# A fused attention and two-expert kernel: VectorE closes the old chunk before it finishes the new one

## The chip, the cores and the metric

The kernel runs on one core of one Trainium2 chip. The metric is device time in microseconds (us) for one execution. Engines are called as in the profile: PE (TensorE), PEld (its weight loads), DVE (VectorE), ACT (ScalarE), POOL (GpSimd) and SP (SyncE, which here issues DMAs). L340 means line 340 of the kernel before.

## The reference

The program computes a windowed causal attention with a linear bias (4 batches, 8 heads, 576 positions, head size 64), reshapes its output to 2304 tokens of 512 features, and sends these through two pairs of dense layers. Only the first pair matters here:

```python
def _moe_ref(x, w_in, w_out, a, b):
    h = x @ w_in                       # 2304 x 512 by 512 x 2048
    h2 = h * h
    h3 = h2 * h
    P = a[0] + a[1] * h + a[2] * h2 + a[3] * h3
    Q = 1.0 + np.abs(b[0]) * np.abs(h) + np.abs(b[1]) * h2
    g = P / (Q + 1e-06)
    return g @ w_out                   # 2304 x 2048 by 2048 x 512
```

The second pair has the same sizes, `g = h` where `h > 0` and `exp(h) - 1` elsewhere.

## The kernel before, in words

Full precision on PE comes from splitting every operand into a rounded high part and a low remainder, and multiplying hi·hi, lo·hi and hi·lo. So a product of 128 rows by a contraction of 512 takes 12 matmuls.

The tokens of the first pair are cut into five blocks (512, 512, 512, 256, 512). In each block the 2048 hidden features are cut into 16 chunks of 128, so there are 80 chunks, counted c or s over all blocks, and f = 0 to 15 in a block. For every chunk PE makes a first product (`gemm1`, L287: 12 matmuls into the bank `h`) and a second one (`gemm2_T`, L725: 12 matmuls that add to four `acc` banks). Between the two stands `rational`, the quotient P/(Q + 1e-6), on 128 x 512 tiles.

One call `rational(c)` works on two chunks at once, the new chunk c and the old chunk c - 1:

- ACT makes of the new `h`: its square h2 (L311), qa = |b0|·|h| (L312), ee = a0 + a1·h (L313), and a2 + a3·h in place of h (L314). Then the reciprocal of Q as exp(-ln Q): L325 and L326, into `rr`.
- DVE makes for the old chunk the rounded quotient hi = ee0·rr0 (L319), then qq0 = Q·hi (L331), then the remainder ee0 - qq0 (L339). POOL (DVE for the first four chunks) multiplies that by rr0 (L340): this is the low part of the quotient.
- DVE makes for the new chunk Q without its 1 (L322), h2 times the rest of the polynomial (L336, into `h`), and adds that to ee (L337).

The tiles `ee` and `qq` exist twice and lie in a token block of `xT` that is used up; a chunk takes the pair of the chunk before the last. So L313 of the next chunk writes the tile that POOL reads in L340, and waits for it. `h2` exists once, so L311 of the next chunk waits for L336. The order on each engine is the order in which the program text issues (`manual_schedule`). PE runs ahead: in the loop over s it issues `gemm1(s)`, then `gemm2_T(s - 3)`, then `rational(s)` is issued to the other engines.

Between these passes stand jobs on weights. In block 0 they convert this pair's weights (`conv_step`, L138, L148, L156 to L162). In blocks 1 and 2 all chunks but f = 0, 8 and 15 have two "joins": 26 chunks, 52 joins. A join takes half of a weight slice of the second pair: ACT scales its high words (L130), DVE shifts its low words (L138), then ORs both (L800), SP stores the result and loads a further half. The first join of a chunk stands between L319 and L322; the second one's shift stands before L331, and its L800 (which needs an L130 that ACT makes after L326) after L331. At f = 15, ACT and DVE also split the next block's x into hi and lo (`split_x`, L268 and L269), and three chunks later ACT copies the four `acc` banks of the finished block (L732).

After the 80 chunks the second pair of layers runs with a planner of its own, which the diff doesn't touch.

Of the kernel before, what the change touches and what calls it, by code (L numbers as in the profile page):

```python
# [13 lines left out]
ALU = mybir.AluOpType  # L14
# [30 lines left out]
def kernel(  # L45
# [13 lines left out]
    nc = tc.nc  # L59
# [178 lines left out]
    def width(c):  # L238
        return BL[c // KF][1]

    def row1(tag, c):

        t0, n = BL[c // KF]
        if tag in BESIDE:
            return xT[:, BESIDE.index(tag), t0:t0 + n]
        where, c0 = ROW1[tag]
        return SPACE[where][:, c0:c0 + n]
# [5 lines left out]
    def bank(n, shape, name):  # L253
        return psum.tile(shape, F32, tag=f"b{n}", name=name)
# [47 lines left out]
    def rational(c, old=True, beside=3 * (lambda: None,), after=lambda: None):  # L302


        old = old and c - 1 in q_t
        new = c in h_t
        if new:
            h = h_t.pop(c)
            h2, ee, qq, rr = [row1(nm, c) for nm in ("h2", f"ee{c % 2}", f"qq{c % 2}", f"rr{c % 2}")]
            qa = bank(6, [P, width(c)], "qa") if c > 3 else qq  # L310
            nc.scalar.activation(out=h2, in_=h, func=AF.Square)  # L311
            nc.scalar.activation(out=qa, in_=h, func=AF.Abs, scale=b_abs[:, 0:1])  # L312
            nc.scalar.activation(out=ee, in_=h, func=AF.Identity, scale=a_sb[:, 1:2], bias=a_sb[:, 0:1])  # L313
            nc.scalar.activation(out=h, in_=h, func=AF.Identity, scale=a_sb[:, 3:4], bias=a_sb[:, 2:3])  # L314
        if old:
            qq0, ee0, rr0 = q_t.pop(c - 1)
            hi, low = row1(f"ghi{c % 3}", c - 1), row1(f"glo{c % 3}", c - 1)
            g_t[c - 1] = (hi, low)
            nc.vector.tensor_tensor(out=hi, in0=ee0, in1=rr0, op=ALU.mult)  # L319
        beside[0]()  # L320
        if new:
            nc.vector.scalar_tensor_tensor(  # L322
                out=qq, in0=h2, scalar=b_abs[:, 1:2], in1=qa, op0=ALU.mult, op1=ALU.add
            )
            nc.scalar.activation(out=rr, in_=qq, func=AF.Ln, bias=c_q)  # L325
            nc.scalar.activation(out=rr, in_=rr, func=AF.Exp, scale=-1.0)  # L326
            q_t[c] = (qq, ee, rr)
        after()
        beside[1]()
        if old:  # L330
            nc.vector.scalar_tensor_tensor(  # L331
                out=qq0, in0=qq0, scalar=EPSC, in1=hi.bitcast(F32), op0=ALU.add, op1=ALU.mult
            )
        beside[2]()
        if new:
            nc.vector.tensor_tensor(out=h, in0=h2, in1=h, op=ALU.mult)  # L336
            nc.vector.tensor_tensor(out=ee, in0=ee, in1=h, op=ALU.add)  # L337
        if old:
            nc.vector.tensor_tensor(out=ee0, in0=ee0, in1=qq0, op=ALU.subtract)  # L339
            (nc.gpsimd if c > 4 else nc.vector).tensor_tensor(out=low, in0=ee0, in1=rr0, op=ALU.mult)  # L340


    def attention():
        with ExitStack() as es:
# [339 lines left out]
            for t in range(first, NU + 2):  # L684
                if 0 <= t < 12:
                    load_some(2)
                if t == NU - 1:
                    x1[0] = split_x(0, "DADA")
                    ahead = early()
                for step, late in STEPS:  # L690
                    run(step, t + late)
                    if t < NU - 1 or not 0 <= t + late < NU:
                        continue

                    for _ in range(AHEAD.get((t + late, step), 0)):
                        next(ahead, None)
                    if (t + late, step) in CONV_AFTER:
                        conv_step(to_conv, to_conv[0] not in LATE[4:], eng="D")
                    if (t + late, step) == FIRST["r0"]:
                        rational(0)  # L700
                    if (t + late, step) == FIRST["r1"]:
                        rational(1, old=False)
                if t == 0:
                    nc.sync.dma_start(out=a_sb, in_=moe_a.partition_broadcast(P))
                    nc.sync.dma_start(out=b_raw, in_=moe_b.partition_broadcast(P))
                if t == 2:
                    nc.scalar.activation(out=b_abs, in_=b_raw, func=AF.Abs)
# [3 lines left out]
    def experts():  # L711
# [519 lines left out]
        def prepare(s):  # L1231
            f = s - LAST
            if f == 3:
                load_wi(0)
            if f == 14:
                load_wi(1)
                for e in raw_ones(0):
                    load_raw(0, e)

            def copies():  # L1240
                for fn in AT_ACT.get(f, []):
                    fn()

            def next_one():
                if f >= 3 and AT_DVE:
                    AT_DVE.pop(0)()
            rational(s, beside=(lambda: None, next_one, next_one), after=copies)
# [89 lines left out]
```

## Time and profile before

| | |
|---|---|
| runs | 980.41, 980.75, 981.29 us; median 980.75 |
| the profiled execution | 981.41 us, of which 979.6 us span from the first to the last instruction |
| PE busy | 927.1 us (95%) |
| DVE busy | 824.5 us (84%) |
| ACT busy | 709.4 us (72%) |
| POOL busy | 192.8 us (20%) |
| mean granted clock of PE | 0.995 of full speed |

The times are of a whole execution. The span leaves out 1.8 us around it. PE is busy nearly always, but the share is a mean: the attention, the five blocks and the second pair have different limits. In the trace the blocks lie about here: block 0 from 150 to 230 us, block 1 to 341, block 2 to 455, block 3 to 510 and block 4 to 597.

### The profile page before, as it was taken

Reading aid. Unit: us, or ns where it says so; the run is one execution under the profiler, and the core shown is the slowest. Engines: PE = TensorE matmul, PEld = TensorE weight load, DVE = VectorE, ACT = ScalarE, POOL = GpSimd, SP = SyncE. Lnnn points to the kernel's source line nnn. Section 1 sums busy time; section 2 is a strip of 40 time slices with the busy share of each in tenths; the row PEclk is TensorE's granted clock in tenths of the full one; section 3 lists DMA queues with packets and bytes.
Section 4 is the critical chain, followed back from the end, with each engine's and each line's share of the span. In section 5 each row is a group of like instructions: output and inputs, shape, how many; then the busy total and the mean of one; then the engine's idle time right before and its main releaser. Section 6 shows DMA issues by size and latency. Waiting matters only on the chain.

```text
span 979.6 us, 15614 instructions
## 1 busy us (share of the span) xinstructions
PE 927.1 (95%) x5110; PEld 775.1 (79%) x5110; DVE 824.5 (84%) x1773; ACT 709.4 (72%) x1510; POOL 192.8 (20%) x238
## 2 busy tenths in 40 slices
PE   9999999999888797878999999999999999999998
PEld 6777777877666586657988888899998999899897
DVE  7899999999888888887789998999978878787653
ACT  6999998778666676666787787767776657676553
POOL 4566650222222122222222321000000000000000
PEclk9999999999999999998999999999999999999999
DMA  8999851011333223230000012435444232343201
GB/s 163 226 261 216 216 152 41 1 33 33 102 92 105 89 82 113 81 114 22 1 2 32 1 64 77 148 121 194 129 147 145 85 118 76 124 155 109 75 1 65
DMA packets 112561, 98.28 MB, mean 100 GB/s; under 512 B 62816, under 2 KB 86368, under 8 KB 112480
## 3 DMA queue, kind: packets, MB, share of 16 engines
q1 hardware_dynamic: 109936, 96.57, 33.6%
q10 hardware_dynamic: 2544, 0.72, 0.4%
q8 instruction: 40, 0.66, 0.3%
q14 instruction: 41, 0.34, 0.1%
HBM read 79.96 MB, written 17.30 MB: 99 GB/s over the span
## 4 chain that ended last, share of the span: by engine, by line
PE 59%; DVE 21%; issue 6%; ACT 6%; POOL 4%; DMA 2%; POOLq 0%; DVEq 0%; ACTq 0%
PE acc L951 20%; PE m L935 18%; PE acc L725 9%; PE h L287 8%; POOL space_g L340 4%; DVE h L336 2%; DVE xT L337 2%; DVE xT L339 2%; ACT xT L313 2%; DVE half L138 2%; ACT h L314 1%; DVE pr_wi L518 1%; DMA joined_wi<-space_u 1%; DVE cvt L148 1%; DVE pr_wo L518 1%
## 5 line engine op out<-in xcount | busy, mean ns | idle before, releaser
L725 PE MATMUL acc<-space_g,w_wo 128*128 128x512 f32 (+1 forms) x960 | 222.7, 375 | 32.1 <-POOL space_g L340 30.4
L725 PEld LDWEIGHTS acc<-space_g,w_wo 128*128 128x128 f32 x960 | 168.8, 190 | 74.1 <-POOL space_g L340 43.2
L340 POOL TENSOR_TENSOR space_g<-xT,space_r 128x512 fp32r<-128x512 f32 (+1 forms) x76 | 106.3, 1399 | 348.0 <-DVE xT L339 281.1
L313 ACT ACTIVATE xT<-h,a_sb 128x512 f32<-128x512 f32 (+1 forms) x80 | 59.0, 738 | 82.7 <-POOL space_g L340 81.6
L951 PE MATMUL acc<-op_wo,space_g 128*128 128x512 f32 x432 | 108.3, 393 | 0.0
L287 PE MATMUL h<-space_qa,w_wi 128*128 128x512 f32 (+1 forms) x320 | 92.3, 372 | 4.0 <-ACT space_qa L268 3.3
L951 PEld LDWEIGHTS acc<-op_wo,space_g 128*128 128x128 f32 x432 | 80.4, 188 | 14.7
L287 PE MATMUL h<-space_qb,w_wi 128*128 128x512 f32 (+1 forms) x240 | 76.6, 374 | 3.8 <-DVE space_qb L269 3.6
L997 ACT ACTIVATE space_u<-space_r 128x384 f32<-128x384 f32 x48 | 25.1, 522 | 75.3 <-DVE space_r L991 74.3
L287 PE MATMUL h<-space_ta,w_wi 128*128 128x512 f32 (+1 forms) x240 | 77.0, 375 | 2.3 <-DVE space_ta L269 2.3
L935 PE MATMUL m<-xo_wi,op_wi 128*128 128x384 f32 x336 | 77.3, 337 | 0.0
L935 PE MATMUL m<-xo_wo,op_wi 128*128 128x384 f32 x336 | 76.4, 335 | 0.0
L287 PEld LDWEIGHTS h<-space_qa,w_wi 128*128 128x128 f32 x320 | 57.4, 189 | 15.5 <-ACT space_qa L268 4.8
L336 DVE TENSOR_TENSOR h<-space_u,h 128x512 f32<-128x512 f32 (+1 forms) x80 | 51.0, 637 | 16.8 <-ACT h L314 16.7
L935 PEld LDWEIGHTS m<-xo_wo,op_wi 128*128 128x128 f32 x336 | 60.9, 188 | 4.1
L325 ACT ACTIVATE space_r<-xT,c_q 128x512 f32<-128x512 f32 (+1 forms) x80 | 54.2, 678 | 11.2 <-DVE xT L322 8.6
L935 PEld LDWEIGHTS m<-xo_wi,op_wi 128*128 128x128 f32 x336 | 60.6, 188 | 0.0
L322 DVE SCALAR_TENSOR_TENSOR xT<-space_u,b_abs,qa 128x512 f32<-128x512 f32 (+1 forms) x76 | 52.1, 686 | 10.0 <-ACT qa L312 10.0
L287 PE MATMUL h<-space_bi,w_wi 128*128 128x512 f32 (+1 forms) x160 | 59.6, 373 | 0.0
L311 ACT ACTIVATE space_u<-h 128x512 f32<-128x512 f32 (+1 forms) x80 | 43.7, 546 | 21.6 <-DVE h L336 19.0
L1001 ACT ACTIVATE space_u<-space_u,c_m 128x384 f32<-128x384 f32 x96 | 57.5, 610 | 1.6
L331 DVE SCALAR_TENSOR_TENSOR xT<-xT,space_g 128x512 f32<-128x512 f32 (+1 forms) x80 | 57.9, 723 | 0.1
(187 smaller groups left out, 2158.7 us busy)
## 6 DMA issues: line engine op xcount, KB each, us to landing
space_qa<-joined_wo SPq DMA_DIRECT2D x43, 256.0 KB, 2.7
raw_wo<-in_moe_w_out_dram SPq DMA_DIRECT2D x20, 512.0 KB, 5.0
raw_wi<-in_moe_w_in_dram SPq DMA_DIRECT2D x16, 512.0 KB, 4.2
half<-in_moe_w_in_dram SPq DMA_DIRECT2D x32, 256.0 KB, 2.7
two_wo<-joined_wi SPq DMA_DIRECT2D x32, 256.0 KB, 2.9
s<-sums SPq DMA_DIRECT2D x32, 256.0 KB, 2.8
half<-in_moe_w_out_dram SPq DMA_DIRECT2D x22, 256.0 KB, 2.8
v<-in_v_dram SPq DMA_DIRECT2D x32, 128.0 KB, 3.5
```

Source lines behind the costliest of these rows:

```text
L287: nc.tensor.matmul(h, lhsT=WT["wi", f][:, SEL[wp], kk * P:(kk + 1) * P], rhs=x[xp][kk], start=(kk == 0 and n == 0), stop=(kk == KD - 1 and ...
L311: nc.scalar.activation(out=h2, in_=h, func=AF.Square)
L313: nc.scalar.activation(out=ee, in_=h, func=AF.Identity, scale=a_sb[:, 1:2], bias=a_sb[:, 0:1])
L322: nc.vector.scalar_tensor_tensor(out=qq, in0=h2, scalar=b_abs[:, 1:2], in1=qa, op0=ALU.mult, op1=ALU.add)
L325: nc.scalar.activation(out=rr, in_=qq, func=AF.Ln, bias=c_q)
L331: nc.vector.scalar_tensor_tensor(out=qq0, in0=qq0, scalar=EPSC, in1=hi.bitcast(F32), op0=ALU.add, op1=ALU.mult)
L336: nc.vector.tensor_tensor(out=h, in0=h2, in1=h, op=ALU.mult)
L340: (nc.gpsimd if c > 4 else nc.vector).tensor_tensor(out=low, in0=ee0, in1=rr0, op=ALU.mult)
L725: nc.tensor.matmul(acc_t[d], lhsT=WT["wo", f][:, SEL[wp], d * P:(d + 1) * P], rhs=gt[SEL[xp]], start=(f == 0 and n == 0), stop=(f == KF - ...
L935: nc.tensor.matmul(out, lhsT=w[:, SEL[wp], c0:c0 + P], rhs=XO[q // NP2, nm, k][:, SEL[xp]], start=(k == 0 and n == 0), stop=(k == 1 and n ...
L951: nc.tensor.matmul(acc_t[T, t], lhsT=gt[SEL[xp]][:, t * P:(t + 1) * P], rhs=w[:, SEL[wp]], start=(first and n == 0), stop=(last and n == 2),)
L1001: nc.scalar.activation(out=e, in_=e, func=AF.Identity, bias=c_m)
```

## The change

In the last part of `rational`, the two passes of the new chunk (L336, L337) and the two of the old chunk (L339 and L340) change places. No instruction is added or taken away. The new lines 336 and 337 are the old 339 and 340, and the new 339 and 340 are the old 336 and 337. The condition names no width, so the 256-token block is changed too. All text below uses the numbers of the kernel before.

```diff
         beside[2]()
+        if old:
+            nc.vector.tensor_tensor(out=ee0, in0=ee0, in1=qq0, op=ALU.subtract)
+            (nc.gpsimd if c > 4 else nc.vector).tensor_tensor(out=low, in0=ee0, in1=rr0, op=ALU.mult)
         if new:
             nc.vector.tensor_tensor(out=h, in0=h2, in1=h, op=ALU.mult)
             nc.vector.tensor_tensor(out=ee, in0=ee, in1=h, op=ALU.add)
-        if old:
-            nc.vector.tensor_tensor(out=ee0, in0=ee0, in1=qq0, op=ALU.subtract)
-            (nc.gpsimd if c > 4 else nc.vector).tensor_tensor(out=low, in0=ee0, in1=rr0, op=ALU.mult)
```

DVE in block 1, one chunk with two joins, from its second L800 to the first join of the chunk after it, before the change. `space_u` holds h2 (and the first join's words), `space_w` the second join's words, `xT` stands for the tiles ee and qq.

```order
L800 SCALAR_TENSOR_TENSOR space_w_2421<-space_w_2421,half_3375 128x256
L336 TENSOR_TENSOR h<-space_u,h 128x512
L337 TENSOR_TENSOR xT<-xT,h 128x512
L339 TENSOR_TENSOR xT<-xT 128x512
L319 TENSOR_TENSOR space_g<-xT,space_r_76 128x512
L138 TENSOR_SCALAR half_3385<-half_3385 128x256
```

The same place after the change, with the line numbers of the changed kernel (L336 there is the remainder, L339 and L340 are the new chunk's passes):

```order
L800 SCALAR_TENSOR_TENSOR space_w_2421<-space_w_2421,half_3375 128x256
L336 TENSOR_TENSOR xT<-xT 128x512
L339 TENSOR_TENSOR h<-space_u,h 128x512
L340 TENSOR_TENSOR xT<-xT,h 128x512
L319 TENSOR_TENSOR space_g<-xT,space_r_76 128x512
L138 TENSOR_SCALAR half_3385<-half_3385 128x256
```

The remainder, after which POOL may begin, moved up by two passes; the pass that reads the sum of the new chunk (L319) now follows that sum directly.

DVE in block 1 at f = 8, the one inner chunk without joins, before the change, from L319 to the L319 of the next chunk:

```order
L319 TENSOR_TENSOR space_g<-xT,space_r_76 128x512
L322 SCALAR_TENSOR_TENSOR xT<-space_u,b_abs,qa 128x512
L331 SCALAR_TENSOR_TENSOR xT<-xT,space_g 128x512
L336 TENSOR_TENSOR h<-space_u,h 128x512
L337 TENSOR_TENSOR xT<-xT,h 128x512
L339 TENSOR_TENSOR xT<-xT 128x512
L319 TENSOR_TENSOR space_g<-xT,space_r_75 128x512
```

And after it:

```order
L319 TENSOR_TENSOR space_g<-xT,space_r_76 128x512
L322 SCALAR_TENSOR_TENSOR xT<-space_u,b_abs,qa 128x512
L331 SCALAR_TENSOR_TENSOR xT<-xT,space_g 128x512
L336 TENSOR_TENSOR xT<-xT 128x512
L339 TENSOR_TENSOR h<-space_u,h 128x512
L340 TENSOR_TENSOR xT<-xT,h 128x512
L319 TENSOR_TENSOR space_g<-xT,space_r_75 128x512
```

Here the remainder follows directly on the pass that makes its operand qq0 (L331). The rows of ACT, POOL, PE and SP stand in the same order in both kernels.

## Rows read from the trace of the kernel before

**Rows 1.** Busy time by stage: engine busy us (instructions), granted clock, DMA share, GB/s.
```profile
200.00:460.00 260.00, 221.29 (x932) 173.41 (x931) 224.85 (x358) 175.82 (x312) 61.15 (x40) 0.98 0.26 82
```

**Rows 2.** Waits, whole span: engine line <- releaser: total us, times, longest.
```profile
ACT xT L313 <- POOL space_g L340: 81.6, 62, 1.9
...
PE acc L725 <- POOL space_g L340: 30.4, 23, 1.5
...
PE h L287 <- DVE space_qb L269: 3.6, 2, 1.9
...
PE h L287 <- ACT space_qa L268: 3.3, 4, 1.0
...
PE h L287 <- DVE space_ta L269: 2.3, 4, 0.7
```

**Rows 3.** Timeline of a chunk with two joins, block 1: start us, us, engine, line.
```profile
294.23 0.78 ACT L313 ACTIVATE xT<-h,a_sb 128x512 f32<-128x512 f32 x1 [1.17 <-POOL space_g L340]
294.45 0.42 DVE L800 SCALAR_TENSOR_TENSOR space_u<-space_u,half 128x256 int32<-128x256 int32 x1
294.79 0.74 DVE L322 SCALAR_TENSOR_TENSOR xT<-space_u,b_abs,qa 128x512 f32<-128x512 f32 x1
...
295.45 0.29 DVE L138 TENSOR_SCALAR half<-half 128x256 int32<-128x256 int32 x1
295.57 0.72 ACT L325 ACTIVATE space_r<-xT,c_q 128x512 f32<-128x512 f32 x1
...
296.32 0.63 ACT L326 ACTIVATE space_r<-space_r 128x512 f32<-128x512 f32 x1
296.86 0.42 ACT L130 ACTIVATE space_w<-half 128x256 f32<-128x256 f32 x1
...
297.31 0.43 DVE L800 SCALAR_TENSOR_TENSOR space_w<-space_w,half 128x256 int32<-128x256 int32 x1 [0.97 <-ACT space_w L130]
297.65 0.69 DVE L336 TENSOR_TENSOR h<-space_u,h 128x512 f32<-128x512 f32 x1
...
298.37 0.69 DVE L337 TENSOR_TENSOR xT<-xT,h 128x512 f32<-128x512 f32 x1
298.43 0.60 ACT L311 ACTIVATE space_u<-h 128x512 f32<-128x512 f32 x1 [0.84 <-DVE h L336]
...
298.93 0.66 ACT L312 ACTIVATE qa<-h,b_abs 128x512 f32<-128x512 f32 x1
298.98 0.68 DVE L339 TENSOR_TENSOR xT<-xT 128x512 f32<-128x512 f32 x1
...
299.58 0.68 DVE L319 TENSOR_TENSOR space_g<-xT,space_r 128x512 fp32r<-128x512 f32 x1
299.83 1.55 POOL L340 TENSOR_TENSOR space_g<-xT,space_r 128x512 fp32r<-128x512 f32 x1 [5.64 <-PE h L287]
300.18 1.35 DVE L138 TENSOR_SCALAR half<-half 128x256 int32<-128x256 int32 x1
301.42 0.78 ACT L313 ACTIVATE xT<-h,a_sb 128x512 f32<-128x512 f32 x1 [1.83 <-POOL space_g L340]
...
301.64 0.43 DVE L800 SCALAR_TENSOR_TENSOR space_u<-space_u,half 128x256 int32<-128x256 int32 x1
```

**Rows 4.** Timeline of POOL and DVE side by side, chunk f = 8.
```profile
287.38 1.56 POOL L340 TENSOR_TENSOR space_g<-xT,space_r 128x512 fp32r<-128x512 f32 x1 [5.64 <-DVE xT L339]
287.73 0.74 DVE L322 SCALAR_TENSOR_TENSOR xT<-space_u,b_abs,qa 128x512 f32<-128x512 f32 x1
288.39 1.10 DVE L331 SCALAR_TENSOR_TENSOR xT<-xT,space_g 128x512 f32<-128x512 f32 x1
```

**Rows 5.** Chain that ended last, early in block 2: start us, us, what.
```profile
349.55 2.72 PE h L287 x12
352.27 2.73 PE acc L725 x12
```

**Rows 6.** Timeline of ACT just after: the copies of the finished block.
```profile
352.99 2.64 ACT L732 ACTIVATE xT<-acc 128x512 f32<-128x512 f32 x4 [0.64 <-PE acc L725]
```

## The prediction

> **What bounds the kernel now.** I read the busy time by stage first, then the list of waits, then the timeline of one chunk of the stage that waits. In the first the reader is to see that blocks 1 and 2 hold the idle time of PE: from 200 to 460 us it is busy 221.29 of 260 us, 38.7 us idle [rows 1]. The waits say for whom: 30.4 us in 23 waits of the second product (L725) for POOL's low part (L340), and 3.6 + 3.3 + 2.3 = 9.2 us of the first product (L287) for the hi and lo parts of the next block's x, at the block boundaries [rows 2]. So up to 39.6 us of PE time can be had, no more; outside these stages PE has hardly anything to win.
>
> The timeline shows why POOL is late. A chunk with joins takes 7.19 us, from one L313 (294.23) to the next (301.42) [rows 3], while PE needs 2.72 + 2.73 = 5.45 for its two products [rows 5]. The 7.19 are a closed loop, step by step from start to start [rows 3]: L313 to L325 1.34, to L326 0.75, to the join's L130 0.54, to the second L800 0.45, to L336 0.34, to L337 0.72, to L339 0.61, to POOL 0.85, to the next L313 1.59. The sum is 7.19: every step waits for the one before. ACT's L313 waits for POOL 81.6 us in all [rows 2], since POOL still reads the tile that it overwrites; POOL waits for L339, which stands behind the two passes of the new chunk, and these need L314, behind L313.
>
> **The change, part by part.** Nothing is added or removed; DVE alone gets another order, and no DMA changes its place. Three things move.
>
> First, the remainder (L339) comes two passes earlier, so POOL does too. It now starts 1.19 us behind the second L800 (0.34 to L339, 0.85 to POOL) where it started 2.52 us behind it (299.83 - 297.31) [rows 3].
>
> Second, POOL meets other neighbours. Now L319 starts just before it and runs to 300.26, 0.43 us into POOL's 1.55 [rows 3]. In the other direction, DVE passes that start while POOL runs are drawn out: L138 takes 1.35 instead of 0.29 us [rows 3], and L331, in the chunk without joins, takes 1.10, to 0.55 us past POOL's end at 288.94 [rows 4]. But L322, which started in the same POOL instruction, took 0.74, as long as at 294.79 without POOL [rows 3, 4]. L322 reads one operand from PSUM; L331 and L319 read both from SBUF. L336 and L337 read `h` from PSUM like L322, so I take it that they neither delay POOL nor are delayed. POOL then takes 1.55 - 0.43 = 1.12 us, and ends at 2.31.
>
> The Trainium skill ("SBUF — State Buffer", section "Who interferes with whom") says the same: a VectorE instruction with two SBUF inputs contends with a GpSimd one that reads SBUF, one with at most one SBUF input doesn't, and whichever issues first holds the shared port for the whole instruction. The pair of 0.74 and 1.10 agrees. By its last part L319 would pay in full if it began just before POOL's end; that is a rival below.
>
> Third, L336 and L337 come 0.60 and 0.57 us later, L336 now at 0.94 and L337 at 1.66. L311 of the next chunk waits for L336 (it came 0.09 behind its end [rows 3]), and L319 follows L337 with a dependence: I give it the 0.72 of L336 to L337 instead of 0.61.
>
> The new round, from the second L800 = 0 on DVE: L339 0.34, L336 0.94, L337 1.66, L319 2.38, L138 2.98 (0.60 behind it, as before). POOL has ended, so L138 takes its 0.29, and L800 comes 0.11 behind its end, as at 301.53 to 301.64: 3.38. Then L322 3.72 (0.34), L325 4.50 (0.78), L326 5.25, L130 5.79 and the second L800 at **6.24** [steps of rows 3]. The two other ways through are earlier: L311 at 1.72, L312 at 2.22 to 2.88, so L322 at 3.72 doesn't wait for it (0.84 us of cover); L313 behind that at about 2.9 no longer waits for POOL's 2.31, and 2.9 + 1.34 = 4.24 is before L325's 4.50. So the loop through POOL is cut, and a shorter one through DVE is left: 6.24 us a chunk, 0.79 over PE's 5.45.
>
> The inner chunk without joins: from L319 at 2.38, L322 +0.60, L331 +0.66, L339 +0.72 (now directly dependent), POOL +0.85, so 5.21, and POOL to POOL 5.21 - 1.19 = 4.02. It gives PE 1.43 us of reserve back.
>
> What PE then waits, by the reserve (how long POOL's low part lies ready before PE wants it). Three chunks into a block ACT copies the finished `acc` banks. That ends at 355.63, 0.63 behind PE's end at 355.00 [rows 5, 6], and only then can ACT start on the new chunk. From there to POOL's end: L311 0.63, L312 0.50, its end 0.66, L322 to L325 0.78, 0.75, 0.54, 0.45, then 2.31: 6.62 us. PE wants that low part after three products (8.17) and two matmuls that use the hi part (2 x 2.73 / 12 = 0.45): 8.62. The reserve is 2.0. Five chunks at 0.79 eat it up and leave a wait of 1.9; f = 8 gives 1.43 back; five more (f = 9 to 13) take 3.95, of which 2.5 are waited. The wait for f = 14 falls behind the boundary. So 1.9 + 2.5 = 4.4 us a block, 8.8 for blocks 1 and 2, in place of 30.4: **-21.6 us**.
>
> The boundaries I leave at 9.2. The first should lose its share, as block 0 (no joins, and shifts that POOL no longer blocks) stops falling behind; at the two others PE still comes with no reserve, and the lo parts stand behind L337, now the last pass, so their wait is a little longer. Blocks 3 and 4 and the second pair of layers: zero, PE covers them. If that cover failed, a dependent step costs 0.11 a chunk, 32 chunks, 3.5 us.
>
> Against the profiled execution's 981.41 us this makes 959.8. The median of the runs is 0.66 below that execution, so 959.1.
>
> **Bounds.** The one price that no row shows is L336 and L337 beside POOL. At best POOL's part vanishes from PE altogether, with the boundaries: -39.6, 941. At worst they behave like L138, 1.06 a chunk more, and nothing is won. I take the L322 row, nearest in kind (PSUM operand, same width).
>
> **The rivals.**
>
> 1. L319 loses the port. It starts at 2.38, POOL ends at 2.31; a POOL that runs its 1.55 whatever its neighbours ends at 2.74. L319 would then grow as L331 did, by 1.10 - 0.69 = 0.41, and the round is 6.65, 1.20 over PE. Per block: five chunks 6.0 - 2.0 = 4.0, f = 8 gives 1.0 back, five more 5.0: 9.0, together 18.0. Gain 12.4, time 968.3. For it: POOL's records are 1.55 to 1.56 wide; against: L319's overlap explains the 0.43.
>
> 2. The round is shorter than PE's, because steps that I added overlap. Then the 30.4 go whole, and some of the boundaries' 9.2: 946 to 950. For it: in the round now DVE stands idle for 0.97 before its second L800 [rows 3], so it has room; against: the dependence from L800 through L325 to the next L800 has each step from rows.
>
> 3. No effect: the change doesn't do what it says, since L313 still waits, for another reader of its tile. The reason against it is that the only older readers are L339 and L340, which both came forward. 980.7.
>
> 4. Slower: POOL is starved. If POOL can't start between back-to-back DVE passes, as it now gives way to L319 for 0.43, it waits for L336, L337 and L319, to 3.06, and ends at 3.06 + 1.12 = 4.18 behind the L800, where it now ends at 4.07 (301.38 - 297.31). Each of the 26 chunks with joins pays 0.11, 2.9 us: 983.6. This decides if L336 and L337 contend in spite of their PSUM operand; the L322 row speaks against it.
>
> **How the numbers follow.** The forecast, 955 to 964 by itself, has 0.58; rival 1 (964 to 970) 0.18; rival 2 0.13; rival 3 0.05; rival 4 0.06. The range 946 to 970 takes in the first three. A measurement of this kernel can tell 0.2% (2 us) from no change. Faster by more than that has 0.58 + 0.18 + 0.13 = 0.89, within it 0.05, slower 0.06.
>
> **What would show it.** In the profile of the changed kernel: POOL's start every 6.2 us in the chunks with joins; its record near 1.1 us; L138 at 0.29 in both joins; the wait of L313 for POOL (81.6) nearly gone; the wait of L725 for POOL near 9 us. Wrong it would be if POOL's pace stayed at 7.2, if L336 or L337 took over 0.9 us beside POOL, or if the wait of PE came back at the boundaries in the size that the chunks lost.

## The result and the profile after

| | before | after |
|---|---|---|
| runs, us | 979.91 to 981.29, median 980.58 (4 runs) | 946.77 to 951.53, median 948.51 (4 runs) |
| ratio, 95% interval | | 0.9676 (0.9650 to 0.9702) |
| the profiled execution | 981.41 us, span 979.6 | 951.53 us, span 949.7 |

The change makes the kernel 32.1 us faster, where 21.5 were forecast (959.1); the time lies in the range (946 to 970), but below the band that the forecast itself was given (955 to 964) and inside that of rival 2 (946 to 950). The profiled execution of the changed kernel is its slowest run.

The waits after the change, same columns as in [rows 2]. L337 is the old L340:

```profile
PEld acc L725 <- POOL space_g L337: 15.1, 16, 1.1
...
PE acc L725 <- POOL space_g L337: 8.3, 16, 0.7
...
PE h L287 <- DVE space_qb L269: 3.8, 2, 2.0
PE h L287 <- ACT space_qa L268: 3.4, 2, 1.8
```

The wait of L313 for POOL, 81.6 us before, is not among them. PE waits 8.3 us for POOL in place of 30.4; 8.8 was forecast. At the boundaries 9.2 us became 7.2.

One round of a chunk with two joins after the change, block 1, second L800 to second L800, as in [rows 3]. L336 is the remainder, L339 and L340 are the new chunk's passes:

```profile
273.99 0.43 DVE L800 SCALAR_TENSOR_TENSOR space_w<-space_w,half 128x256 int32<-128x256 int32 x1 [0.98 <-ACT space_w L130]
274.33 0.68 DVE L336 TENSOR_TENSOR xT<-xT 128x512 f32<-128x512 f32 x1
274.93 0.69 DVE L339 TENSOR_TENSOR h<-space_u,h 128x512 f32<-128x512 f32 x1
275.18 1.28 POOL L337 TENSOR_TENSOR space_g<-xT,space_r 128x512 fp32r<-128x512 f32 x1 [5.04 <-DVE xT L336]
275.65 0.69 DVE L340 TENSOR_TENSOR xT<-xT,h 128x512 f32<-128x512 f32 x1
275.71 0.60 ACT L311 ACTIVATE space_u<-h 128x512 f32<-128x512 f32 x1 [1.44 <-DVE h L339]
...
276.45 0.69 DVE L319 TENSOR_TENSOR space_g<-xT,space_r 128x512 fp32r<-128x512 f32 x1
276.78 0.78 ACT L313 ACTIVATE xT<-h,a_sb 128x512 f32<-128x512 f32 x1
277.06 0.29 DVE L138 TENSOR_SCALAR half<-half 128x256 int32<-128x256 int32 x1
...
277.45 0.43 DVE L800 SCALAR_TENSOR_TENSOR space_u<-space_u,half 128x256 int32<-128x256 int32 x1
277.79 0.74 DVE L322 SCALAR_TENSOR_TENSOR xT<-space_u,b_abs,qa 128x512 f32<-128x512 f32 x1
...
278.57 0.72 ACT L325 ACTIVATE space_r<-xT,c_q 128x512 f32<-128x512 f32 x1 [0.36 <-DVE xT L322]
...
279.32 0.63 ACT L326 ACTIVATE space_r<-space_r 128x512 f32<-128x512 f32 x1
279.86 0.41 ACT L130 ACTIVATE space_w<-half 128x256 f32<-128x256 f32 x1
280.31 0.43 DVE L800 SCALAR_TENSOR_TENSOR space_w<-space_w,half 128x256 int32<-128x256 int32 x1 [0.97 <-ACT space_w L130]
```

The round is 280.31 - 273.99 = 6.32 us; 6.24 was forecast, 7.19 stood in [rows 3]. L313 has no idle time ahead of it any more. The two passes that run beside POOL (L339 and L340 here) take 0.69 as before, and POOL's record is 1.28 instead of 1.55. L138 takes 0.29 where it took 1.35. L319 begins as POOL ends (276.45 against 275.18 + 1.28), here and in the other joined chunks.

Where the time went, from the starts of PE's second products (L725) in both traces:

| stretch | before, us | after, us | difference |
|---|---|---|---|
| attention, to the first L725 | 154.44 | 158.46 | +4.02 |
| block 0 and the boundary behind it | 74.87 | 71.81 | -3.06 |
| block 1 | 98.82 | 87.16 | -11.66 |
| boundary of blocks 1 and 2 | 23.98 | 22.90 | -1.08 |
| block 2 | 86.82 | 76.61 | -10.21 |
| boundary of blocks 2 and 3 | 17.03 | 14.87 | -2.16 |
| block 3 | 46.33 | 42.92 | -3.41 |
| boundary of blocks 3 and 4 | 6.50 | 4.18 | -2.32 |
| the rest | 470.8 | 470.8 | 0.0 |

The sum is -29.9, the difference of the spans (949.7 - 979.6). Blocks 1 and 2 gave 21.9 us, almost the 21.6 forecast. Another 12.0 us came from stretches that were put at nothing: the boundaries with block 0 (8.6) and block 3 (3.4). The attention, which the change doesn't touch, was 4.0 us later in this execution. Its trace shows why: PE's granted clock had a mean of 0.77 from 35 to 50 us, against 1.00 in the kernel before. The figures are PE busy, then PEld, DVE, ACT and POOL, then the granted clock; first before, then after:

```profile
35.00:50.00 15.00, 14.27 (x147) 10.55 (x144) 14.08 (x59) 14.55 (x48) 7.60 (x15) 1.00 0.93 229
```

```profile
35.00:50.00 15.00, 13.57 (x101) 10.19 (x99) 10.52 (x45) 10.69 (x33) 4.68 (x9) 0.77 0.92 210
```

A mean of 0.77 over 15 us loses some 3.4 us of PE's time at full clock (an estimate).

### The profile page after: what moved, and what is told of

Same layout as the page of the kernel before. It is cut to its first block, busy times and chain, and to the rows that moved or that the text cites. A ratio compares the mean times of both kernels' runs of the same rounds, so it can differ in the third digit from the quotient of the medians.

```text
span 949.7 us, 15573 instructions
## 1 busy us (share of the span) xinstructions
PE 920.9 (97%) x5110; PEld 776.2 (82%) x5110; DVE 787.3 (83%) x1773; ACT 710.8 (75%) x1510; POOL 175.9 (19%) x238
## 4 chain that ended last, share of the span: by engine, by line
PE 70%; DVE 19%; DMA 4%; ACT 3%; issue 2%; DVEq 0%; SPq 0%; ACTq 0%
PE acc L951 21%; PE m L935 18%; PE acc L725 14%; PE h L287 13%; DVE space_g L319 2%; DVE xT L340 2%; DVE xT L336 2%; DVE h L339 2%; DVE pr_wi L518 1%; DMA joined_wi<-space_u 1%; DVE pr_wo L518 1%; DMA v<-in_v_dram 1%; DVE cvt L148 1%; DMA joined_wo<-space_u 1%; PE s_ps L492 1%
## 5 line engine op out<-in xcount | busy, mean ns | idle before, releaser
L725 PE MATMUL acc<-space_g,w_wo 128*128 128x512 f32 (+1 forms) x960 | 217.2, 372 | 9.1 <-POOL space_g L337 8.3
L725 PEld LDWEIGHTS acc<-space_g,w_wo 128*128 128x128 f32 x960 | 168.5, 190 | 46.0 <-POOL space_g L337 15.1
L337 POOL TENSOR_TENSOR space_g<-xT,space_r 128x512 fp32r<-128x512 f32 (+1 forms) x76 | 89.4, 1176 | 329.3 <-DVE xT L336 239.3
L287 PE MATMUL h<-space_qa,w_wi 128*128 128x512 f32 (+1 forms) x320 | 91.9, 371 | 4.1 <-ACT space_qa L268 3.4
L287 PE MATMUL h<-space_qb,w_wi 128*128 128x512 f32 (+1 forms) x240 | 76.1, 371 | 3.8 <-DVE space_qb L269 3.8
L287 PE MATMUL h<-space_ta,w_wi 128*128 128x512 f32 (+1 forms) x240 | 76.1, 372 | 0.0
L287 PEld LDWEIGHTS h<-space_qa,w_wi 128*128 128x128 f32 x320 | 57.5, 189 | 15.0 <-ACT space_qa L268 4.2
L322 DVE SCALAR_TENSOR_TENSOR xT<-space_u,b_abs,qa 128x512 f32<-128x512 f32 (+1 forms) x76 | 52.2, 687 | 16.6 <-ACT qa L312 16.4
L325 ACT ACTIVATE space_r<-xT,c_q 128x512 f32<-128x512 f32 (+1 forms) x80 | 55.1, 689 | 13.7 <-DVE xT L322 13.4
L287 PE MATMUL h<-space_bi,w_wi 128*128 128x512 f32 (+1 forms) x160 | 59.6, 372 | 0.0
L319 DVE TENSOR_TENSOR space_g<-xT,space_r 128x512 fp32r<-128x512 f32 (+1 forms) x80 | 51.4, 643 | 9.5 <-PE h L287 0.5
L313 ACT ACTIVATE xT<-h,a_sb 128x512 f32<-128x512 f32 (+1 forms) x80 | 59.3, 741 | 0.0
L1001 ACT ACTIVATE space_u<-space_u,c_m 128x384 f32<-128x384 f32 x96 | 57.5, 611 | 1.6
L314 ACT ACTIVATE h<-h,a_sb 128x512 f32<-128x512 f32 (+1 forms) x80 | 57.4, 717 | 0.0
```

The lines of the kernel that those rows point to most:

```text
L287: nc.tensor.matmul(h, lhsT=WT["wi", f][:, SEL[wp], kk * P:(kk + 1) * P], rhs=x[xp][kk], start=(kk == 0 and n == 0), stop=(kk == KD - 1 and ...
L322: nc.vector.scalar_tensor_tensor(out=qq, in0=h2, scalar=b_abs[:, 1:2], in1=qa, op0=ALU.mult, op1=ALU.add)
L725: nc.tensor.matmul(acc_t[d], lhsT=WT["wo", f][:, SEL[wp], d * P:(d + 1) * P], rhs=gt[SEL[xp]], start=(f == 0 and n == 0), stop=(f == KF - ...
L1001: nc.scalar.activation(out=e, in_=e, func=AF.Identity, bias=c_m)
```

## The experiments

"Round" below is POOL's start to start in the inner chunks with joins. Each kernel's ratio is to the kernel before, on the same chip. The edits are shortened: "remainder, POOL" stands for the old chunk's two closing passes and "h2 * h, ee + h" for the new chunk's, with the kernel before's line numbers. `KF` is 16, the chunks of a block.

**The new order in the joined chunks of blocks 1 and 2 alone.** The old order stands everywhere else:

```
+        first = KF <= c < 3 * KF and c % KF not in (0, KF // 2, KF - 1)
         if first: close_old()        # L339, L340
         if new: ...                  # L336, L337
         if not first: close_old()
```

> The new order only in the 26 chunks of blocks 1 and 2 that have joins, the old order in all others. Theory (a closed loop L313 - second L800 - L336 - L337 - L339 - POOL - L313 sets the pace of these chunks, and the change cuts it): POOL's pace in them falls from 7.19 to 6.32 us as in the full change, PE's start gains 21.9 us there and some 3 us at the two boundaries behind these blocks; block 0, block 3 and its boundary stay as before (PE's pace of 3.21 us in block 3): 955 to 959 us. Rival (the gain is in blocks 0 and 3, and blocks 1 and 2 only shift): over 970 us.

Measured: 958.87 us, ratio 0.9769 (0.9745 to 0.9792). The round is 6.32, PE's pace in block 3 stays at 3.21 and at the first boundary at 7.7. Blocks 1 and 2 give 20.6 us, where the change gave 21.9, and the boundaries behind them 2.4. So these 26 chunks carry most of the gain, and the rival is out.

**The new order in block 3 alone**, `first = 3 * KF <= c < 4 * KF`.

> The new order only in the 256-token block (c = 48 to 63), the old one in all others. Theory (there too the loop through POOL sets the pace, 3.21 us a chunk, though PE's records show it busy): PE's pace falls to 2.88, 3.4 us over the block, and with the boundary behind it 5.7 us: 974 to 977 us. Rival (PE is busy all of that block, so its own work bounds it, as the prediction took it): 980 to 981 us.

Measured: 975.92 us, ratio 0.9941 (0.9921 to 0.9961); PE's pace falls from 3.21 to 2.88, and the boundary behind the block from 6.5 to 4.18. Together with the run before this makes 22.6 + 5.5 = 28.1 us; block 0, which had no run of its own, gave 3.1 in the table above. Busy time by stage over the block's inner part, first the kernel before, then this one (PE busy, PEld busy):

```profile
462.00:502.00 40.00, 39.26 (x303) 37.02 (x302) 28.60 (x72) 31.39 (x77) 8.42 (x12) 1.00 0.00 1
```

```profile
462.00:497.00 35.00, 35.00 (x289) 34.81 (x288) 28.66 (x72) 31.91 (x78) 8.88 (x12) 1.00 0.00 1
```

PE counts as busy in 98% of the first stretch too, yet 303 matmuls in 40 us are 7.6 a us, against 289 in 35 us, 8.3. The weight loads (PEld) show more of it, with 37.02 of 40 us against 34.81 of 35. The 0.33 us a chunk lie inside the records: two rows of that block in the kernel before show it, where the second product of 12 matmuls takes 1.94 us; a row of the changed kernel has 1.60.

```profile
479.82 1.94 PE L725 MATMUL acc<-space_g,w_wo 128*128 128x256 f32 x12
...
480.27 0.56 ACT L313 ACTIVATE xT<-h,a_sb 128x256 f32<-128x256 f32 x1 [0.73 <-POOL space_g L340]
```

```profile
448.81 1.60 PE L725 MATMUL acc<-space_g,w_wo 128*128 128x256 f32 x12
```

The second of the rows before is the sign that I passed over: the same wait of L313 for POOL, every 3.21 us.

**POOL one pass later than in the change.** The remainder and POOL's pass stand between the two passes of the new chunk:

```
         if new: h2 * h               # L336
+        if old: remainder, POOL      # L339, L340
         if new: ee + h               # L337
```

> All blocks: the remainder (L339) and POOL's pass stand between the two passes of the new chunk, one pass later than in the change. Theory with the port (a DVE pass with both operands in SBUF waits for a POOL pass that has begun): POOL begins 1.79 us behind the second L800 and ends at 3.08, L319 comes at 2.27 and is drawn out to over 1.1 us, the round is 6.6 to 6.9 us, PE waits some 18 us for POOL, time 955 to 962 us. Rival (only POOL's distance from L313 counts, and that is not what binds any more): L319 stays at 0.69, round 6.3, 947 to 950 us as the change.

Measured: 960.93 us, ratio 0.9786 (0.9762 to 0.9809); round 6.78, PE's wait for POOL 17.5 us. Its timeline at L319 (L338 is the remainder, L341 the sum, L339 POOL's pass):

```profile
268.19 0.68 DVE L341 TENSOR_TENSOR xT<-xT,h 128x512 f32<-128x512 f32 x1
...
268.44 1.27 POOL L339 TENSOR_TENSOR space_g<-xT,space_r 128x512 fp32r<-128x512 f32 x1 [5.51 <-DVE xT L338]
268.97 1.28 DVE L319 TENSOR_TENSOR space_g<-xT,space_r 128x512 fp32r<-128x512 f32 x1
```

L319, both operands in SBUF, began 0.53 us into POOL's pass and took 1.28 instead of 0.69; POOL's own record stayed at 1.27, and L341 with an operand in PSUM was not touched. So rival 1 of the prediction names a real price, which this order pays and the change doesn't. The Trainium skill ("SBUF — State Buffer", section "Who interferes with whom") has issue order decide who is blocked. L319 agrees: 1.28 us behind POOL's start here, 0.68 in [rows 3], where it began 0.25 us ahead of POOL.

**The changed kernel again.**

> The changed kernel once more, for its spread. If the 4.0 us by which its profiled execution was later at the end of the attention (an unchanged part) were an accident of that execution, another one reaches the first L725 at 154.5 us and takes 946 to 948 us; if they came from the change, it again reaches it at 158.5 us.

Measured: 948.91 us, ratio 0.9666 (0.9645 to 0.9687). The profiled execution reached the first L725 at 155.10 us, with a span of 946.3. Its granted clock from 35 to 50 us is 1.00. The 4.0 us in the attention belonged to one execution.

**L313 freed of POOL, old order.** The remainder goes to the tile of the low part, so POOL no longer reads ee0 (it is rounded once more by that):

```
-            nc.vector.tensor_tensor(out=ee0, in0=ee0, in1=qq0, op=ALU.subtract)
-            ....tensor_tensor(out=low, in0=ee0, in1=rr0, op=ALU.mult)
+            nc.vector.tensor_tensor(out=low, in0=ee0, in1=qq0, op=ALU.subtract)
+            ....tensor_tensor(out=low, in0=low.bitcast(F32), in1=rr0, op=ALU.mult)
```

> The old order, but L339 writes the remainder into the tile of the low part, and POOL multiplies it there, so L313 no longer waits for POOL (the remainder is rounded once more by it). Theory of two loops (in joined chunks the loop through L313 and a second one through the port, POOL - first L138 - L800 - L322 - L325 - L326 - L130 - second L800 - L336 - L337 - L339 - POOL, are equally long): the round of a chunk with joins stays at 7.2 us, and the wait of PE for POOL near 25 to 30 us; only block 0 and block 3 gain, time 970 to 977 us. Rival (the wait of L313 is all that bound it): the round falls to 6.3 or less and the time to 950 us or less.

Measured: 972.30 us, ratio 0.9903 (0.9886 to 0.9919). In most joined chunks the round stays at 7.25 to 7.29 us, and PE's wait for POOL is 29.1 us, though L313 waits no more. The gain lies where no joins stand: block 0 with its boundary 3.1 us, block 3 3.3 (its pace is 2.88), the boundary behind it 2.3. There freeing L313 alone removes the loss, so that loop alone was the bound. Its timeline from POOL's pass to the second L800:

```profile
263.83 1.58 POOL L340 TENSOR_TENSOR space_g<-space_g,space_r 128x512 fp32r<-128x512 f32 x1 [5.68 <-DVE space_g L339]
264.20 1.36 DVE L138 TENSOR_SCALAR half<-half 128x256 int32<-128x256 int32 x1
...
265.66 0.43 DVE L800 SCALAR_TENSOR_TENSOR space_u<-space_u,half 128x256 int32<-128x256 int32 x1
266.00 0.74 DVE L322 SCALAR_TENSOR_TENSOR xT<-space_u,b_abs,qa 128x512 f32<-128x512 f32 x1
...
266.84 0.72 ACT L325 ACTIVATE space_r<-xT,c_q 128x512 f32<-128x512 f32 x1 [1.70 <-DVE xT L322]
```

ACT stands idle for 1.70 us ahead of L325, for L322, which stands behind the L138 that POOL drew out to 1.36. That is a second loop through POOL, as long as the first.

**The first join behind L322, old order.** L322 then doesn't wait for the blocked L138; L313 still waits for POOL:

```
-    beside=(first_join, lambda: join_shift(nj + 1), ...)
+    beside=(lambda: None, lambda: (first_join(), join_shift(nj + 1)), ...)
```

> The old order, but the first join of a chunk (L138, L800) stands behind L322 instead of before it, so that L322 and with it L325 no longer wait for the L138 that POOL blocks. Theory of two loops: the loop through L313 stays, round 7.2 us, time 979 to 982 us. Rival (the port alone bound it): round 6.3 or less, 955 us or less.

Measured: 980.89 us, ratio 0.9992 (0.9983 to 1.0002): no difference. Round 7.19, the wait of L313 81.1 us.

**Both edits together**, still the old order.

> The old order with both edits: remainder in the tile of the low part, and the first join behind L322 (the remainder is rounded once more). Theory of two loops: with both cut the round falls to about 5.85 us, PE's wait for POOL to a few us, time 942 to 950 us, although neither edit alone moves these chunks. Rival (something else binds, as the order of L339 behind L336 and L337): round 7.2 us, time as e4.

Measured: 941.63 us, ratio 0.9587 (0.9565 to 0.9609), the round 5.88. In the joined chunks one edit gives nothing and both give 1.3 us a round: two loops of one length, and both had to go. It also shows that the order L336, L337, L339 as such isn't the bound. The time is just under the 942 to 950 that I had expected. What is left in the joined chunks is L325's wait for POOL, 0.33 us in most of them; the two long waits of L325 for L322 (2.8 and 2.3) stand at the boundaries:

```profile
ACT space_r L325 <- POOL space_g L340: 12.6, 34, 1.3
ACT space_r L325 <- DVE xT L322: 12.2, 12, 2.8
```

**All closing passes ahead of the second join's L800, new order.**

```
+        if old: remainder, POOL
+        if new: h2 * h, ee + h
         beside[2]()                  # the second join's L800
-        if old: ...
-        if new: ...
```

> The new order, and all four closing passes issued before the second join's L800 instead of behind it. Theory: L800 leaves the loop, which is then L319 0, L138 0.60, L800 1.0, L322 1.34, L331 2.2, L339 2.92, L336 3.52, L337 4.24, second L800 4.85, drawn out a little by POOL, next L319 5.4 to 5.5: no more than PE's 5.44. PE's wait for POOL goes to under 2 us and the time 8 to 11 us below the changed kernel, 936 to 941 us. Rival (another order moves the wait only: the second L800 collides with POOL and costs 1 us a chunk): 947 us or more.

Measured: 923.93 us, ratio 0.9414 (0.9400 to 0.9428), the best of all. PE doesn't wait in blocks 1 and 2, nor at a boundary, and its pace is 5.44 in every chunk of these blocks:

```profile
200.00:430.00 230.00, 230.00 (x1108) 194.44 (x1108) 207.40 (x397) 193.36 (x354) 55.14 (x46) 1.00 0.31 92
```

In the profiled execution of the changed kernel the same stretch holds 914 matmuls at a busy time of 214.56:

```profile
200.00:430.00 230.00, 214.56 (x914) 171.31 (x913) 188.17 (x348) 172.12 (x303) 49.00 (x38) 0.99 0.29 92
```

I had expected 936 to 941; against the second run of the changed kernel, blocks 1 and 2 gave 11.4 us, a little over the 8 to 11 expected, and the two boundaries behind them 13.0 more, which the last experiment explains.

**Only the old chunk's passes ahead of the second join's L800.**

> The new order, and only the old chunk's two passes (L339, L340) issued before the second join's L800; the new chunk's two stay behind it. POOL then starts about 1.5 us earlier in the round than in the change. Theory of the port: the second L800 has both operands in SBUF and becomes ready just after POOL has begun, so it is held to POOL's end (its record grows from 0.43 to over 1.2 us), and it stands in the loop that sets the pace: round 6.9 to 7.2 us, PE waits over 20 us for POOL, time 960 to 972 us, slower than the change. Rival (the earlier POOL starts, the better): round 6.3 or less and 948 us or less.

Measured: 958.98 us, ratio 0.9769 (0.9749 to 0.9790), so 10 us slower than the change, though POOL starts earlier. The round is 6.77, a little under what I expected, as is the time; PE's recorded wait for POOL is 13.5 us, not over 20; the waits of L287 at the boundaries have grown to 10.5 us. Its timeline (L336 is POOL's pass):

```profile
271.41 1.26 POOL L336 TENSOR_TENSOR space_g<-xT,space_r 128x512 fp32r<-128x512 f32 x1 [5.50 <-PE h L287]
271.49 1.46 DVE L800 SCALAR_TENSOR_TENSOR space_w<-space_w,half 128x256 int32<-128x256 int32 x1 [0.25 <-ACT space_w L130]
```

The second L800 came 0.08 us behind POOL's start and took 1.46 instead of 0.43. "The earlier POOL, the better" falls.

**The changed kernel with a reserve at the boundaries.** DVE's join passes are left out at f = 11 to 14 of blocks 1 and 2, so these weight slices are stored unjoined. The other joined chunks keep their passes:

```
+                if f > 10:
+                    def no_words(n):
+                        keep_half(n)
+                        load_half(n + 3)
+                    rational(s, ..., beside=(lambda: no_words(nj), lambda: None, lambda: no_words(nj + 1)))
```

> The changed kernel, with VectorE's four join passes (two L138, two L800) left out in the last four joined chunks before each of the two boundaries behind blocks 1 and 2 (f = 11 to 14); L130 and the DMAs stay, so these weight slices are stored unjoined. The order at the boundary itself is as in the change. Theory (PE waits at a boundary because it comes there with no reserve): the 7.1 us of waits of L287 at the two boundaries go to under 1.5 us, and the waits for POOL in the same chunks go too: 936 to 941 us. Rival (the boundary has a cost of its own, hi and lo parts that stand behind the closing passes): L287 still waits 5 to 7 us there, 943 to 946 us.

Measured: 931.52 us, ratio 0.9486 (0.9470 to 0.9502). L287 doesn't wait at either boundary any more. Busy time by stage at the boundaries, of the second run of the changed kernel and of this one (PE busy first, then the other engines; PE's granted clock behind POOL):

```profile
320.00:330.00 10.00, 8.20 (x30) 6.44 (x29) 9.73 (x17) 7.66 (x14) 2.57 (x2) 0.83 0.14 39
...
420.00:430.00 10.00, 8.68 (x42) 7.68 (x43) 9.56 (x19) 7.24 (x15) 3.37 (x3) 0.83 0.03 9
```

```profile
305.00:325.00 20.00, 20.00 (x90) 16.53 (x90) 18.95 (x31) 18.93 (x34) 5.22 (x4) 1.00 0.33 96
400.00:420.00 20.00, 20.00 (x113) 17.51 (x112) 15.45 (x30) 16.55 (x35) 4.63 (x4) 1.00 0.15 46
```

A boundary's wait is a lack of reserve, not a cost of the split, whose order is the same in both kernels. The kernel with all closing passes ahead of the join leaves no pass out and has no wait there either. And it costs more than its wait. From the starts of L725, the two boundaries take 13.0 us more in the second run of the changed kernel (paces of 11.87, 5.55, 9.80 and 5.04 against 5.44, 5.44, 4.15 and 4.19); 7.2 of these are waits of L287 and 1.1 waits of L725 for POOL. Right after those waits the granted clock's mean is 0.83 over 10 us, that is, PE worked part of the time at the lower of its two levels (1.2 GHz): 1.7 us lost at each boundary, 3.4 in all (an estimate). About 1.3 us no row accounts for.

## Why the prediction was right, and where it was too small

- **The loop through POOL** sets the pace of the joined chunks: right. It was a pair of loops, though. The prediction walked only the one through L313; the other, through the L138 that POOL blocks, it named as a drawn-out pass and not as a bound. Freeing L313 alone left the round at 7.25 to 7.29, moving the join alone left it at 7.19. The forecast came out because the change cuts both, and because its new round was walked afresh, with L138 at 0.29. In blocks 0 and 3 the loop through L313 was the only one.
- **The new round**, 6.24: right, 6.32. L319 comes 0.80 behind the sum (275.65 to 276.45), not 0.72, and that is the whole difference. It begins just as POOL ends; whether POOL held it for these 0.08 us no run shows. (L337 comes 0.60 later by the prediction's own figures, not 0.57; its sum uses 0.60.)
- **L336 and L337 beside POOL cost nothing**: right, 0.69 each. POOL beside them takes 1.28, not 1.12: the overlap of 0.43 with L319 had cost it 0.27.
- **The reserve**: right in size for PE's recorded wait, 8.3 for 8.8, and for the gain of blocks 1 and 2, 21.9 for 21.6. Here luck helped. By PE's pace these blocks lay 33.3 us over 5.44 a chunk before and 11.5 after, so the 30.4 and the 8.8 are both nearly 3 us too low, and their difference holds.
- **"The boundaries I leave at 9.2"**: this step failed. Together with block 0 they gave 8.6 us. The waits fell by only 2.0 as recorded; the rest is the pace inside and behind them. The prediction had itself expected the first boundary's share to go, and set against it a longer wait at the next two. The recorded waits of L287 there did grow, from 6.8 to 7.2 us, but those of L725 for POOL in the same stretches fell from 2.9 to 1.1, and the two stretches became 1.08 and 2.16 us shorter. Some 1.7 of the 2.16 is the clock (an estimate): its mean over 10 us was 0.66 before and is 0.83. The boundary of blocks 3 and 4, which the prediction didn't treat, gave 2.32. The experiment with a reserve shows the cause: a boundary costs what the chunks ahead of it lack.
- **"Blocks 3 and 4: zero, PE covers them"**: this failed for block 3, 3.4 us, and with its boundary 5.7. The busy share of PE was read as its bound; the block ran at 3.21 us a chunk by POOL's loop, and 2.88 is PE's own pace. The 3.5 us that the prediction named for a failing cover was a loss; the block gained. For block 4 it was right.
- **"Up to 39.6 us of PE time can be had, no more"**: wrong for the same reason. The waits that a view records are no upper bound where records of busy time hide waits and the clock falls behind them: the kernel with all closing passes ahead of the join gained 57.5 us (981.47 to 923.93).
- **The rivals**: the round as short as PE's (rival 2) was not what happened, though the time lies in its 946 to 950, by another way: the boundaries and block 3. L319 losing the port (at most the 0.08 above), and POOL starved, didn't come about; no effect is out.

## What to carry to other kernels

Where a chunk's pace repeats to 0.01 us, walk the loop that sets it, and then look for a second one of the same length through the same late engine: an edit that cuts one of them gains nothing there. Before a stage is put at zero because PE is busy in it, compare its pace with that of the same product in a stage where PE waits for nobody. And when a pass on the second engine is moved, see which pass with two SBUF operands will come to stand beside it: placing that one ahead of or behind it was worth more here than starting it early.

## What the runs showed of the hardware

- A POOL product of 128 x 512 takes 1.28 us when no DVE pass with two SBUF operands overlaps it, 1.55 when one began 0.25 us ahead; a DVE pass with two SBUF operands (or L138, which shifts in place) that becomes ready during it ends 0.1 to 0.6 us after it, whatever its own length: L138 1.36 for 0.29, L319 1.28 for 0.69, L800 1.46 for 0.43. Passes with one operand in PSUM keep 0.68 to 0.74.
- Two waits of PE of 1.6 to 2.0 us at a boundary were followed by a lower granted clock, with a mean of 0.83 in the two rows above; without the waits it stayed at 1.00. In the kernel before, one such stretch (445 to 455 us) stood at 0.66.
- PE's records swallow short waits: 0.33 us of each chunk in block 3 stood inside records of busy time.
